# Two more of the seven outer products of three down groups by inner products, h sums and x added by accumulating transfers

## The chip, the cores and the metric

The kernel runs on one core of a Trainium2 chip. The metric is the device time of one execution, in microseconds. The core has five engines that run their own instruction streams and wait for each other by semaphores: TensorE (PE in the profile, with its weight loads as PEld), VectorE (DVE), ScalarE (ACT), GpSimd (POOL) and SyncE (SP), which in this kernel only issues transfers. Matmuls write to PSUM, which has 8 banks of 128 x 512 float32 numbers.

## The reference

```python
def _A_ref(x, wqkv, wo):                      # linear attention, 32 heads of 32
    qkv = (x @ wqkv) ...                      # S = 2048, D = 1024
    phi = lambda t: jnp.where(t > 0, t + 1, jnp.exp(t)) + 1e-6
    pq, pk = phi(q), phi(k)
    kv = jnp.einsum("bhsd,bhse->bhde", pk, v)
    z = jnp.einsum("bhsd->bhd", pk)
    num = jnp.einsum("bhqd,bhde->bhqe", pq, kv)
    den = jnp.einsum("bhqd,bhd->bhq", pq, z)[..., None] + 1e-6
    return (num / den) ... @ wo
def _B_ref(x, w_gate, w_up, w_down):          # F = 3584
    return (_silu(x @ w_gate) * (x @ w_up)) @ w_down
x = A_x
xn = _layernorm(x, axis=-1)
s = _A_ref(xn, A_wqkv, A_wo)
g = _silu(_B_ref(xn, B_w_gate, B_w_up, B_w_down))
return x + s * g
```

Inputs and output are bfloat16. The last matrix product, h @ w_down with h = silu(gate) * up, is the one that the change is about; below it is called the down product.

## The kernel before

**Seven products instead of eight.** Every large matrix product is computed as in Strassen's scheme (Winograd's form): both operands are cut into 2 x 2 blocks, seven products of sums of blocks are made, and the four output blocks are sums of these. The products are numbered 1 to 7. Products 1, 2 and 4 take raw blocks of the stationary operand; 5, 6, 7 and 3 take the sums S5, S6, S7 and S3 in the code's names. The moving operand has raw blocks `R00` to `R11` and sums `T1` to `T4`; the table `XOF` says which goes with which number. A `Set` holds the two PSUM banks and the side tiles in which the four output blocks of 128 rows x 512 columns come together: `put1`, `keep1`, `put2`, `put5`, `sum5` and `step` copy or add products out of PSUM with ACT and DVE. Two sets, `w` = 0 and 1, form a `Pair`.

**Inner products.** Some of the outer products are cut once more: a `Joint` makes one outer product for both sets of the pair by seven smaller products with 256 moving columns, in four steps a, b, c, d. Step a makes 1 and 5, b makes 6 and 2, c makes 7 and 3, d makes 4. In the step lists a word such as `7_0` is outer product 7 of set 0 in plain form, `j2c` is step c of the joint product 2, and a leading `n` means the next pair.

**Stages.** First come layer norm, transposes and the k and v products (to some 110 us), then, as pairs over the two halves `p` of the tokens, the q columns and seven column blocks `n` of the gate and the up weights, with the attention output s made in between. The gate's silu goes into a ring of eight tiles (`sg_ring`); for the up block the tile is multiplied in place (`h_done`) and stored to `h_scratch` in DRAM, four tiles (i, j) for each `p` and `n`. At about 534 us begin the four down groups of 512 tokens each (`Group`, `dset`). A group loads four blocks of h, makes S5, S7, S6 and S3 from them on DVE (`mk`), and multiplies with the down weights, whose raw blocks and sums stay in SBUF for all groups. Group 0 is plain; in groups 1 to 3 the products 1, 5 and 2 are joint, with inner sums of h by `inner_stat` for each group (the entries I1, I5, I2 of `todo`) and inner sums of the weights by `inner_move` once, during group 0. `evac` of `dset` ends each output block: ACT makes the silu, DVE multiplies with s (loaded from `s_scratch`), DVE adds x (loaded from the input), and SyncE stores the result. The last product of all, 4_1 of group 3, is made in three column pieces (`pieces`).

**What sets the order.** The host builds a list of operations with their reads and writes and a planner (`Plan.schedule`) orders each engine's list: an operation has a due time `dl` that is worked back from TensorE's order, `urgent` and `boost` move it forward, and at each point the engine takes what is due first among what is ready. TensorE keeps the written order, apart from taking a ready product up to ten operations ahead. `emit` turns the order into instruction streams with semaphore waits. Every name given to `dsem` is one DMA semaphore, and at the end SyncE waits for the final count of each of them. The planner's instructions stand in the profile under the line of the helper that makes them: L230 is every matmul, L237 every transpose, L360 ACT, L370 DVE's tensor_tensor, L373 a transfer on SyncE, L222 a wait.

Of the kernel before, what the change touches and what calls it, by code (L numbers as in the profile page):

```python
# [30 lines left out]
class Plan:  # L31
# [60 lines left out]
    def schedule(self):  # L92
# [29 lines left out]
        while len(order) < total:  # L122
# [37 lines left out]
            if o.sem is not None:  # L160
                free[e] = s + 0.08
# [79 lines left out]
def build_kernel(nc, A_x, A_wqkv, A_wo, B_w_gate, B_w_up, B_w_down, out, WINDOW=10, NWARM=14, NPE=4, LEAD=16.0, CLAMP=1000.0, AHEAD=4.0):  # L241
# [12 lines left out]
    with ExitStack() as es:  # L254
# [27 lines left out]
        TM = Arena("TM", 14 * KB)  # L282
        ident = sbt("ident", [128, 128], FP16)
        ones = sbt("ones", [128, 128], FP16)
        maskbd = sbt("maskbd", [128, 128], FP16)
        Zh = sbt("Zh", [128, NG, 32], FP16)
# [3 lines left out]
        stats = sbt("stats", [128, 4, 2, 6], F32)  # L290
# [7 lines left out]
        h_scr = nc.dram_tensor("h_scratch", [4, 2, 2, 128, NPAIR, 256], FP16)  # L298
# [76 lines left out]

        class Ring:
# [29 lines left out]
        ident_r, ones_r, mask_r, nh_r, eps_r = (named(n) for n in ("ident", "ones", "mask", "nh", "eps"))  # L406
# [81 lines left out]
        class Set:  # L488
# [4 lines left out]
            def __init__(self, ops, evac):  # L493
                self.ops, self.evac, self.direct = ops, evac, None
                self.pieces = ()
# [25 lines left out]
            def put2(self, b):  # L521
                if self.direct is not None:
# [8 lines left out]
            def sum5(self):  # L531
                self.c = balloc()
# [3 lines left out]
            def put5(self, e):  # L536
                self.s5 = s5_ring.take()
                act([bank_r[e]], [self.s5.r], self.s5.ap(F32), ps[e][:, :], ACT.Identity)
                bfree(e)

# [78 lines left out]
        class Pair:  # L619
# [6 lines left out]
            def do(self, w):  # L626
# [8 lines left out]
                for fn in self.at.get({"j2c": "2_0", "j2d": "2_1"}.get(w), ()):  # L635
# [5 lines left out]
        LINK2 = ("nj1a nj5a j2d nj1b nj5b 7_0 4_0 nj1c nj2a 3_1 nj2b nj5c n6_0 7_1 nj5d nj1d 4_1 nj2c n3_0 n6_1"  # L641
                 ).split()
# [6 lines left out]
        def feed(pair):  # L649

            prev = last_pair[0]
            if pair is None or not pair.joint:
                if prev is not None:
                    for w in (REST if "2" in (prev.joint or ()) else TAIL):
# [5 lines left out]
            else:  # L660
                third = [x is not None and "2" in (x.joint or ()) for x in (prev, pair)]
                l2 = LINKD if pair.down else LINK2
                link = LINK if not third[1] else l2 if third[0] else LINK1
                early = REST[:6] if third == [True, False] else [w[1:] for w in l2] if third[0] else ()
# [3 lines left out]
                for w in link:  # L668
                    if w[0] == "n":
                        pair.do(w[1:])  # L670
                    elif prev is not None and w not in prev.did and (w[0] != "j" or "2" in prev.joint):
# [38 lines left out]
        def ln_tile(i):  # L710
# [6 lines left out]
            if i == 1:  # L717
                for o in (o0, o1):
                    o.preds.add(first_var[0])
                    first_var[0].succs.append(o)  # L720
            dve([sA, sB], [mvr], lambda h: h.bn_aggr(mv[:, j, :], stats[:, j, :, :]), 60)
# [7 lines left out]
            if i < 2:  # L729
                for c in (0, 512):  # L730
                    dve([s.r, mvr, rsr], [o.sub(2 * c, KB).r], lambda h, c=c: h.tensor_scalar(  # L731
                        oa[:, c:c + 512], xa[:, c:c + 512], mv[:, j, 0:1], rstd[:, j, :], ALU.subtract, ALU.mult),
                        512, 2.6).urgent = 100.0 - c / 25 - 40 * i
# [85 lines left out]
        KSPLIT = {(0, 1), (2, 1), (0, 0), (2, 0), (1, 0), (1, 1), (3, 1), (5, 1), (3, 0), (5, 0)}  # L819
# [289 lines left out]
        def inner_move(v, kt, at, raw=False, ms=(1, 5, 2)):  # L1109
# [3 lines left out]
            for m, places in zip(ms, at):  # L1113
# [3 lines left out]
                if raw and m != 5:  # L1117
# [15 lines left out]
        SPLIT = {(1, 0, 1, 1), (0, 0, 0, 1), (1, 1, 0, 1), (1, 1, 1, 0), (0, 0, 1, 1), (1, 0, 0, 1), (1, 1, 0, 0), (1, 0, 0, 0), (0, 0, 1, 0), (1, 0, 1, 0)}  # L1133
        RECIP = ((("q", 1, 1), "6_0"), (("g", 2, 0), "6_0"))
        NORM = [(("q", 1, 1), "6_1"), (("g", 1, 0), "2_1"), (("u", 1, 0), "6_0"), (("u", 1, 1), "2_1"), (("u", 2, 0), "6_0"), (("u", 2, 1), "6_0"), (("g", 3, 1), "6_0"), (("u", 3, 0), "6_1")]
# [3 lines left out]
        def joint_of(jstat, xin, n, s0, s1):  # L1139
# [6 lines left out]
            js = {"5": Joint(ops(5), lambda w, b: (s0, s1)[w].put5(b))}  # L1146
            if 2 in xin or n == 7:
# [46 lines left out]
        def recip(p):  # L1194

            db = balloc_part()
            mms, rd = [], [zh_r]
# [46 lines left out]

        sgs = {}
# [11 lines left out]
        def gu_pair(p, kind, n, stats, at):  # L1257
            stat, jstat = stats

# [13 lines left out]
            def h_done(w, i, j):  # L1273
                if w == 0:
# [3 lines left out]
                g = 2 * p + j  # L1278
                dma([s.r], [named("h", g, i, n)], h_scr[g, :, i, :, 2 * n:2 * n + 2, :].rearrange(
                    "h p n t -> p h (n t)"), s.ap(FP16).rearrange("p (h x) -> p h x", h=2),  # L1280
                    dsem("hs%d" % s.k), 256 * KB)

            def ev_u(w):
                def f(i, j, ap, r, bank):
                    o, orr = part(h_slot(i, j), w)
                    act([r], [orr], o, halves(ap), ACT.Identity)
# [85 lines left out]

        def wd_load(nm, urgent):
            k, j = DRAW[nm]
            _, rs, v = DV["T1" if nm == "R01" else nm]
            dma([], rs, v.bitcast(BF16), wd_v[:, k, :, j * 512:(j + 1) * 512], dsem("wd" + nm),
                1792 * KB).urgent = urgent
# [6 lines left out]
        def wd_sum(o, a, b):  # L1384
# [362 lines left out]
```

## Time and profile before

| | us |
|---|---|
| median of 3 runs (lowest, highest) | 707.46 (707.27, 707.83) |
| the profiled execution's own time | 707.21 |
| its span, first to last instruction | 705.5 |
| PE busy | 697.2 |
| DVE busy | 602.8 |
| ACT busy | 420.9 |
| POOL busy | 13.5 |

The span leaves out 1.7 us of the profiled execution that lie around it. In the rows below, a group row reads: line, engine, operation, output <- inputs, shapes, count, then busy time and mean duration in ns, then idle time before it and what ended that. A timeline row begins with the start and the length in us. A matmul's row is longer than its share of the time, because matmuls overlap: the distance from one start to the next is what counts.

### The profile page before, as it was taken

How to read it: one execution, taken by the hardware profiler on the slowest of the kernel's cores; microseconds unless marked ns; L12 is line 12 of the kernel's file. 1: busy time of each engine (PE TensorE's matmuls, PEld its weight loads, DVE VectorE, ACT ScalarE, POOL GpSimd, SP SyncE). 2: the span in 40 equal slices, each digit the busy share in tenths (PEclk: the TensorE clock that was granted, in tenths of full speed). 3: DMA queues.
4: the chain of work that ended last, by engine and by line, in shares of the span. 5: the costliest groups of instructions: out<-in, count | busy, mean ns of one | idle time of the engine just before them, and what ended most of it. 6: DMA issues, size and time to landing. Idle time of an engine off the chain costs nothing.

```text
span 705.5 us, 11626 instructions
## 1 busy us (share of the span) xinstructions
PE 697.2 (99%) x4286; PEld 409.3 (58%) x4311; DVE 602.8 (85%) x1391; ACT 420.9 (60%) x834; POOL 13.5 (2%) x35
## 2 busy tenths in 40 slices
PE   8999999999999999999999999999999999999997
PEld 3544445555555666666666666666664457575754
DVE  6999997667999899898999999779899997766853
ACT  4887545877978868688786577775762122222212
POOL 2111000000000000000000000000000000000000
PEclk9999999999999999999999999999999999999999
DMA  9454113113112325343430252749443754446423
GB/s 308 110 112 99 30 60 120 61 60 122 57 61 87 98 91 154 88 145 96 151 119 1 76 192 85 230 142 317 134 151 134 220 175 158 142 139 226 136 66 93
DMA packets 87161, 88.98 MB, mean 126 GB/s; under 512 B 17728, under 2 KB 83008, under 8 KB 87104
## 3 DMA queue, kind: packets, MB, share of 16 engines
q1 hardware_dynamic: 87104, 88.23, 40.4%
q8 instruction: 34, 0.56, 0.3%
q14 instruction: 23, 0.19, 0.1%
HBM read 61.87 MB, written 23.20 MB: 121 GB/s over the span
## 4 chain that ended last, share of the span: by engine, by line
PE 97%; DVE 1%; DMA 0%; ACT 0%; issue 0%
PE ps L230 97%; DMA W<-in_A_x_dram 0%; DVE W L370 0%; PE ps L237 0%; DVE stats L715 0%; DVE H L808 0%; DVE stats L716 0%; DVE TM L370 0%; ACT X L360 0%; ACT TM L360 0%; ACT H L360 0%; DVE TM L807 0%; ACT ps L360 0%; DVE W L731 0%; ACT W L360 0%
## 5 line engine op out<-in xcount | busy, mean ns | idle before, releaser
L230 PE MATMUL ps<-P,W 128*128 128x512 f16 (+1 forms) x952 | 200.1, 341 | 0.0
L360 ACT ACTIVATE TM<-ps 128x512 f32<-128x512 f32 (+2 forms) x331 | 165.2, 532 | 51.7 <-PE ps L230 50.3
L370 DVE TENSOR_TENSOR ps<-ps,TM 128x256 f32<-128x256 f32 (+1 forms) x304 | 148.2, 508 | 54.9 <-PE ps L230 48.9
L230 PE MATMUL ps<-X,W 128*128 128x512 f16 (+1 forms) x896 | 187.9, 340 | 0.1
L360 ACT ACTIVATE H<-ps 128x512 f16<-128x512 f32 (+1 forms) x181 | 106.7, 601 | 62.5 <-PE ps L230 61.2
L230 PEld LDWEIGHTS ps<-P,W 128*128 128x128 f16 (+1 forms) x952 | 93.1, 98 | 65.5 <-issue 0.2
L230 PEld LDWEIGHTS ps<-X,W 128*128 128x128 f16 (+1 forms) x896 | 87.5, 98 | 58.3
L370 DVE TENSOR_TENSOR W<-W 128x256 f16<-128x256 bf16 (+4 forms) x274 | 98.1, 395 | 12.4 <-ACT W L360 8.9
L230 PE MATMUL ps<-H,W 128*128 128x512 f16 (+3 forms) x475 | 105.6, 357 | 0.8
L360 ACT ACTIVATE ps<-ps 128x256 f32<-128x256 f32 (+2 forms) x143 | 61.5, 430 | 56.7 <-PE ps L230 50.1
L230 PE MATMUL ps<-W 128*128 128x256 f16 x533 | 93.6, 273 | 0.0
L370 DVE TENSOR_TENSOR H<-H 128x1024 f16<-128x1024 f16 (+5 forms) x149 | 85.7, 593 | 7.3 <-ACT H L360 7.2
L230 PE MATMUL ps<-H,X 128*128 128x512 f16 (+4 forms) x383 | 74.3, 340 | 0.6 <-ACT X L360 0.4
L230 PEld LDWEIGHTS ps<-H,W 128*128 128x128 f16 x490 | 47.5, 98 | 45.1 <-ACT TM L360 0.3
L370 DVE TENSOR_TENSOR TM<-ps,TM 128x512 f32<-128x512 f32 x93 | 63.6, 685 | 10.2 <-PE ps L230 9.5
L230 PEld LDWEIGHTS ps<-W 128*128 128x128 f16 (+1 forms) x533 | 52.1, 98 | 29.3 <-ACT TM L360 0.5
L230 PEld LDWEIGHTS ps<-H,X 128*128 128x128 f16 x388 | 36.6, 98 | 32.1 <-ACT X L360 0.5
L230 PE MATMUL ps<-H 128*128 128x256 f16 (+4 forms) x386 | 54.5, 272 | 0.2
L360 ACT ACTIVATE H<-TM 128x512 f16<-128x512 f32 x61 | 38.2, 630 | 8.0 <-DVE TM L370 7.3
L230 PEld LDWEIGHTS ps<-H 128*128 128x128 f16 (+1 forms) x390 | 34.2, 98 | 13.9 <-ACT H L360 0.2
L370 DVE TENSOR_TENSOR H<-ps,TM 128x512 f16<-128x512 f32 (+1 forms) x59 | 40.2, 685 | 2.2 <-PE ps L230 1.8
L230 PE MATMUL ps<-W,H 128*128 128x256 f16 (+1 forms) x230 | 41.9, 317 | 0.0
(89 smaller groups left out, 471.9 us busy)
## 6 DMA issues: line engine op xcount, KB each, us to landing
h_scratch<-H SPq DMA_DIRECT2D x56, 256.0 KB, 3.2
W<-in_B_w_gate_dram SPq DMA_DIRECT2D x7, 1024.0 KB, 5.3
W<-in_B_w_up_dram SPq DMA_DIRECT2D x7, 1024.0 KB, 5.9
H<-in_B_w_down_dram SPq DMA_DIRECT2D x4, 1792.0 KB, 9.1
X<-h_scratch SPq DMA_DIRECT2D x7, 896.0 KB, 5.3
W<-h_scratch SPq DMA_DIRECT2D x5, 896.0 KB, 5.2
W<-in_A_x_dram SPq DMA_DIRECT2D x16, 256.0 KB, 3.2
H<-in_A_wqkv_dram SPq DMA_DIRECT2D x8, 512.0 KB, 8.3
```

The lines of the kernel that those rows point to most:

```text
L230: last = h.matmul(o, l, r, start=st, stop=sp, skip_group_check=True)
L360: op = PL.op("act", reads, writes, lambda h: h.activation(o, i, func, **kw), nel(o) / 1200.0 + (0.055 if src == "ps" else 0.095))
L370: return dve(reads, writes, lambda h: h.tensor_tensor(o, a, b, op), nel(o), 1.92 if fast else 0.96)
```

## The change

- **Joint products.** In groups 1 to 3 the outer products 6 and 3 are joint as well, besides 1, 5 and 2. `Set` gets `third`, `put6` and `put3`; the product sums go through SBUF tiles instead of a third bank. Inner sums I6 and I3 are added for each of these groups, and two more `inner_move` once. The step lists of the down groups (`LINKD`, `RESTD`) are new.
- **Roles exchanged.** In the down product h takes the sums in another arrangement, and the table `DOF` replaces `XOF` for it: the blocks of h are 00, 5, 10, 7 and 11, with 6 = 7 - 00 and 4 = 10 - 6 made by DVE. The tile (0, 1) of h is stored nowhere by itself; it is negated when it is made.
- **h sums by transfers.** Tile (0, 0) is stored twice, as 00 and as 5; tile (1, 1) twice, as 11 and 7; tile (1, 0) once. Tile (0, 1) is then added in DRAM to 5 and to 7 by accumulating transfers, which GpSimd issues (`dacc`).
- **x by transfers.** For groups 0 to 2 six transfers copy x into the output beforehand, and the finished product is added to it by an accumulating transfer. Group 3 keeps the old form, with eight tiles for s and for x.
- **Placement and times.** h slots go from 6 to 4; `ident`, `ones`, `maskbd`, `Zh` and `stats` move into the TM arena; the down weights are loaded in halves, each held back until the third one before it has landed. One warm-up matmul less; at the start the second half of tile 1's statistics comes behind tile 0's normalising. Some jobs (`SPLIT`, `NORM`, `BUILD`) have other places, and the table `BOOST` shifts the due times of some 80 operations. The planner counts a transfer's issue time by its engine.

```diff
-    def build_kernel(... NWARM=14 ...)
+    def build_kernel(... NWARM=13 ...)
...
+        def dacc(reads, writes, o, i, s, nbytes):
+            return PL.op("pool", reads, writes, lambda h: h.dma_start(o, i, accum_op=ALU.add), 1.0, sem=s, nbytes=2 * nbytes)
...
             def keep1(self, a):
-                self.b = a
                 self.s1 = s1_ring.take()
                 act([bank_r[a]], [self.s1.r], self.s1.ap(F32), ps[a][:, :], ACT.Identity)
+                if self.third:
+                    bfree(a)
+                else:
+                    self.b = a
+            def put6(self, b):
+                self.b = b
+                tt([bank_r[b], self.s1.r], [bank_r[b]], ps[b][:, :], ps[b][:, :], self.s1.ap(F32), ALU.add)
+                self.sum5()
...
+            def put3(self, b):
+                d = self.c
+                tt([bank_r[b], d.r], [d.r], d.ap(F32), ps[b][:, :], d.ap(F32), ALU.add)
+                bfree(b)
+                self.evac(0, 1, d.ap(F32), d.r, None)
...
-        LINK2 = ("... nj5d nj1d 4_1 nj2c n3_0 n6_1"
+        LINK2 = ("... nj5d nj1d 4_1 n3_0 nj2c n6_1"
-        LINKD = ("7_0 3_0 nj1a nj1b 7_1 nj5a nj5b 3_1 nj1c nj1d nj2a 4_0 nj5c nj2b nj5d n6_0 4_1 nj2c n6_1 nj2d"
+        LINKD = ("7_0 7_1 j3a j3b 3_0 j3c 4_0 j3d 4_1 3_1 nj1a nj1b nj5a nj5b nj1c nj5c nj1d nj2a nj5d nj2b nj6a nj2c nj6b nj6c nj2d nj6d"
+        RESTD = "j3a j3b 7_0 j3c 4_0 7_1 j3d 4_1".split()
...
             if i == 1:
-                for o in (o0, o1):
-                    o.preds.add(first_var[0])
+                for o, p in ((o0, first_var[0]), (o1, first_var[-1])):
+                    o.preds.add(p)
...
+            if n == 7:
+                js["3"] = Joint(ops(3), lambda w, b: (s0, s1)[w].put3(b))
+                js["6"] = Joint(ops(6), lambda w, b: (s0, s1)[w].put6(b))
...
-                dma([s.r], [named("h", g, i, n)], h_scr[g, :, i, ...], ..., dsem("hs%d" % s.k), 256 * KB)
+                if (i, j) != (0, 1):
+                    for q, nm in enumerate(HAT[i, j]):
+                        r, to = place(nm)
+                        dma([s.r], [r], to, tile(s), dsem("hs%d_%d" % (s.k, q)), 256 * KB)
+                for q, (nm, at) in enumerate((("5", (0, 0)), ("7", (1, 1)))):
+                    if (0, 1) in h_out and at in h_out and (i, j) in ((0, 1), at):
+                        r, to = place(nm)
+                        t = h_out[0, 1]
+                        dacc([t.r, r], [r], to, tile(t), dsem("ha%d_%d" % (t.k, q)), 256 * KB)
...
-        hslots = Slots([(X, 0), (X, 7 * KB), (X, 14 * KB), (X, 21 * KB), (W, 38 * KB), (W, 45 * KB)], 7 * KB)
+        hslots = Slots([(X, 0), (X, 7 * KB), (X, 14 * KB), (X, 21 * KB)], 7 * KB)
-        (g_ring of 3, sl_ring of 3, xo_ring of 4)
+        (g_ring of 3, sl_ring of 2, se_ring of 8, xo_ring of 8)
...
-                self.todo = ["L00", "I1", "L01", "L11", "S5", "I5", "S7", "L10", "S6", "I2", "S3"]
+                self.todo = ["L00", "I1", "L5", "I5", "L10", "I2", "L7", "S6", "I6", "S4", "L11", "I3"]
...
                     act([r], [q.r], qa, ap, ACT.Silu, "ps" if bank is not None else "sb")
                     tt([q.r, tr], [q.r], qa, qa, ta, ALU.mult, True)
+                    if self.g < 3:
+                        dacc([q.r, named("ox", self.g, i)], [named("oo", row, j)], of[row:row + 128, cols], qa,
+                             dsem("oa%d" % q.k), 128 * KB)
+                        return
                     tt([q.r, xr], [xr], xa, qa, xa, ALU.add, True)
                     dma([xr], [], of[row:row + 128, cols], xa, dsem("oo%d_%d" % (x.k, c0)), n * 128)
...
+        for g in range(3):
+            for i in range(2):
+                row = 1024 * (g // 2) + 512 * i + 256 * (g % 2)
+                dma([], [named("ox", g, i)], of[row:row + 256, :], xf[row:row + 256, :], dsem("ox%d%d" % (g, i)),
+                    512 * KB).urgent = 250.0
...
+        for k, v in BOOST.items():
+            PL.ops[k].boost = v
```

More of the change, by code (lines that the diff above doesn't have):

```diff
@@ L160, in schedule @@
             if o.sem is not None:
-                free[e] = s + 0.08
+                free[e] = s + o.busy
                 t0, rate, t1 = self.ALONE if o.start < self.RUSH else self.MIXED
@@ L281, in build_kernel @@
         W = Arena("W", 52 * KB)
[L282 to L286, printed above, removed]
+        TM = Arena("TM", 15 * KB + 512)
+        ident, ones, maskbd = (TM.at(14 * KB + 256 * q, 256, FP16) for q in range(3))
+        Zh = TM.at(14 * KB + 768, 512, FP16).rearrange("p (g n) -> p g n", n=32)
         hmask = sbt("hmask", [128, 4], F32)
@@ L403, in sub @@
                 return Slot(self.a, self.off + off, n, self.k)
-        ident_r, ones_r, mask_r, nh_r, eps_r = (named(n) for n in ("ident", "ones", "mask", "nh", "eps"))
+        ident_r, ones_r, mask_r = (TM.reg(14 * KB + 256 * q, 256) for q in range(3))
+        nh_r, eps_r = named("nh"), named("eps")
         def pool(reads, writes, fn, busy=0.3):
@@ L531, in sum5 @@
             def sum5(self):
+                if self.third:
+                    d = self.c = s1_ring.take()
+                    tt([bank_r[self.b], self.s5.r], [d.r], d.ap(F32), ps[self.b][:, :], self.s5.ap(F32), ALU.add)
+                    return
                 self.c = balloc()
@@ L661, in feed @@
                 third = [x is not None and "2" in (x.joint or ()) for x in (prev, pair)]
-                l2 = LINKD if pair.down else LINK2
-                link = LINK if not third[1] else l2 if third[0] else LINK1
-                early = REST[:6] if third == [True, False] else [w[1:] for w in l2] if third[0] else ()
+                link = LINKD if pair.down else LINK if not third[1] else LINK2 if third[0] else LINK1
+                early = () if pair.down else REST[:6] if third == [True, False] else [w[1:] for w in LINK2] if third[0] else ()
                 for w in REST:
@@ L1285, in f @@
                     o, orr = part(h_slot(i, j), w)
[L1286 removed]
+                    act([r], [orr], o, halves(ap), ACT.Identity, scale=-1.0 if (i, j) == (0, 1) else 1.0)
                     h_done(w, i, j)
```

198 lines of the change are left out of this document (102 added, 96 removed), and 7 rows, old and new, of the table BOOST.

## The prediction

> **What bounds the kernel now.** I read the page first, then the windows, then TensorE's timeline, because the share of busy time says little where matmuls overlap.
>
> ```profile
> span 705.5 us, 11626 instructions
> PE 697.2 (99%) x4286; PEld 409.3 (58%) x4311; DVE 602.8 (85%) x1391; ACT 420.9 (60%) x834; POOL 13.5 (2%) x35
> PE 97%; DVE 1%; DMA 0%; ACT 0%; issue 0%
> 270.00:400.00 130.00, 130.00 (x837) 81.80 (x836) 121.99 (x290) 95.34 (x203) 0.00 (x0) 1.00 0.34 105
> 534.00:591.00 57.00, 56.74 (x311) 30.70 (x315) 56.17 (x94) 12.39 (x24) 0.00 (x0) 1.00 0.44 140
> 591.00:605.00 14.00, 14.00 (x89) 8.54 (x89) 9.06 (x18) 2.23 (x4) 0.00 (x0) 1.00 0.54 179
> 605.00:700.00 95.00, 94.68 (x601) 58.45 (x606) 60.49 (x126) 22.42 (x44) 0.00 (x0) 1.00 0.46 144
> ```
>
> The third line is the chain that ended last, by engine: 97% of it is TensorE. The window rows give length, then busy time of PE, PEld, DVE, ACT and POOL, the granted clock and the DMA share. The clock is 1.00 in each row and PE is never idle by more than 0.4 us a stage, which missing records explain. So from the first product on, the time is the sum of the matmuls; every other engine matters only where it runs late. One engine is close to that: DVE, with 121.99 of 130 us in the gate/up stage and 56.17 of 57 at the start of the down groups.
>
> **The gain: TensorE's work.** Two kinds of product stand side by side in the third down group:
>
> ```profile
> 657.33 0.93 PE L230 MATMUL ps<-H,X 128*128 128x256 f16 x7
> ...
> 661.92 0.93 PE L230 MATMUL ps<-W,X 128*128 128x256 f16 x7
> 662.68 3.19 PE L230 MATMUL ps<-H,X 128*128 128x512 f16 x14
> ...
> 671.05 3.18 PE L230 MATMUL ps<-P,X 128*128 128x512 f16 x14
> 674.07 3.19 PE L230 MATMUL ps<-H,X 128*128 128x512 f16 x14
> 677.09 0.93 PE L230 MATMUL ps<-W,H 128*128 128x256 f16 x7
> ```
>
> Seven groups of 7 narrow matmuls (657.33 to 661.92, then 662.68) take 5.35 us from start to start; that is one whole product done by inner products, 49 of 256 columns. A plain outer product is two groups of 14 wide ones: 671.05 to 677.09, 6.04 us. The change turns products 3 and 6 of groups 1, 2 and 3 from the second kind into the first: 6 x (6.04 - 5.35) = **4.1 us less**. PE has no slack to give this back to, so it is a real gain unless something runs late. Group 0 stays plain. That the edit does less than it says is no case: the new schedule lists hold j3 and j6, and both are built for every group with inner sums.
>
> **The end gets longer.** The last instructions are SyncE's waits, one for every DMA semaphore:
>
> ```profile
> 701.87 0.43 SPq L373 DMA_DIRECT2D out_dram<-TM  x1
> L222 SPq EVENT_SEMAPHORE  x39: 17/28/28, 702.3 to 705.0; - x39
> ```
>
> The second row is line 222 on SyncE in the window 702 to 706. The kernel before uses 78 DMA semaphores (my count of the names), so 39 instructions carry two waits each, and they run one after another from 702.3 to 705.0: 2.7 us over 38 steps, 0.07 us each, all after the last DMA was issued. The names of the new version count to 118: stores of h 8 to 14 and accumulates into h 8 new, loads of h 10 to 8, down weights 4 to 8, s tiles 3 to 10, x tiles 4 to 8, output stores 6 to 10, x copies 6 new, accumulates into the output 3 new; the other 43 stay. That is 20 more instructions on the end, **+1.3 us**. The bounds are 0, if waits already met cost nothing or go elsewhere, and 1.6, if the chain also stalls a second time.
>
> **The last product.** The end order becomes 7_0, j3c, 4_0, 7_1, j3d, 4_1. The last one is cut into column pieces, and its first piece waits for a DVE sum and two ACT copies out of the bank that 7_1 fills:
>
> ```profile
> 691.47 3.19 PE L230 MATMUL ps<-H,X 128*128 128x512 f16 x14
> 691.67 0.69 DVE L370 TENSOR_TENSOR TM<-ps,TM 128x512 f32<-128x512 f32 x1 [1.51 <-PE ps L230]
> 692.40 0.56 ACT L360 ACTIVATE ps<-ps 128x128 f32<-128x128 f32 x2 [3.15 <-DVE TM L370]
> 697.52 3.25 PE L230 MATMUL ps<-H,X 128*128 128x256 f16 x42
> ```
>
> 7_1 gives way at 691.47, the copies are done at 692.96: 1.5 us. Before, 6 us of products covered that. Now only j3d stands behind 7_1, 5.35 / 7 = 0.76 us, so up to 0.8 us of stall. It is 0 if the planner's order of the ready products puts another one there. I take **+0.4**.
>
> **The start.** The normalising of tile 0 no longer queues behind the second half of tile 1's statistics:
>
> ```profile
> 5.46 0.56 POOL L725 TENSOR_TENSOR rstd<-veps,neg_half 128x1 f32<-128x1 f32 x1 [1.50 <-DVE veps L722]
> 6.02 0.68 DVE L716 BATCH_NORM_STATS2 stats<-W 128x6 f32<-128x512 bf16 x1
> 6.61 0.72 DVE L731 TENSOR_SCALAR W<-W,mv,rstd 128x512 f16<-128x512 bf16 x2
> 8.31 0.73 DVE L731 TENSOR_SCALAR W<-W,mv,rstd 128x512 f16<-128x512 bf16 x2 [0.67 <-POOL rstd L725]
> 7.07 0.72 PE L237 MATMUL ps<-ident,W 128*128 128x128 f16 x8 [0.47 <-DVE W L731]
> 8.15 1.04 PE L230 MATMUL ps<-H,X 128*128 128x512 bf16 x4 [0.37 <-ACT X L360]
> 9.03 0.61 PE L237 MATMUL ps<-ident,W 128*128 128x128 f16 x8
> ```
>
> rstd is there at 6.02, so the first product can come up to 0.5 us sooner. But tile 1's normalising then moves from 8.31 to about 8.5, and the transposes at 9.03 wait for it, so most of that is lost again. Bounds -0.5 and 0; I take **-0.1**. The one warm-up matmul less ends in the gap before 7.07 and costs nothing; with that gap gone it would be what the clock loses, which no row here shows.
>
> **The sums moved to transfers.** DVE's pieces for this, and the transfers' own:
>
> ```profile
> L370 DVE TENSOR_TENSOR X<-X 128x1024 f16<-128x1024 f16 x24 | 15.7, 683 | 0.2 <-PE ps L230 0.2
> L370 DVE TENSOR_TENSOR W<-H 128x1792 f16<-128x1792 bf16 x3 | 3.2, 1081 | 0.0
> L370 DVE TENSOR_TENSOR H<-X 128x896 f16<-128x896 f16 x12 | 7.3, 617 | 0.0
> L370 DVE TENSOR_TENSOR TM<-W,TM 128x512 bf16<-128x512 f16 x31 | 12.9, 421 | 0.6
> L370 DVE TENSOR_TENSOR ps<-ps,TM 128x256 f32<-128x256 f32 x18 | 7.7, 429 | 18.0 <-PE ps L230 18.0
> L373 SPq DMA_DIRECT2D h_scratch<-H x56: 359/371/4482, 162.8 to 554.1; - x56
> DMA to landing us min/median/max: 2.1/4.1/10.8
> ```
>
> Per group DVE loses S5 and S7, 2 x (3 x 0.68 + 0.42) = 4.9 us, and in groups 0 to 2 the adding of x, 8 x 0.42 = 3.4. It gains, in groups 1 to 3, inner sums for 6 and 3 (8 x 0.62 = 4.9), four full-width sums (4 x 0.69, from the 691.67 row) and four of 256 columns (1.7): 9.4 against 8.3, about even. Once, around group 0, come 8 block sums of 1.08, 8.6 us. Groups 0 and 1 together: 2 x 8.3 off, 9.4 + 8.6 on, +1.4 us against 4.9 idle in 591 to 605. It fits, but DVE has no pause before 591, so a sum can come late: bounds 0 and 1.0 us, I take **+0.2**. ACT's extra copies fall into 2.23 of 14 and 22.42 of 95 us busy.
>
> On SyncE, stores of h go from 56 to 70 and loads from 16 to 20, 0.37 us of issue each. The down weights come as eight halves instead of four, six copies of x to the output are added, and 24 x loads and 24 output stores go. That is fewer in all, and an earlier place in the queue for those behind. The six copies and the added h traffic cost nothing while the DMA share is 0.34 to 0.54; without that room they would delay a weight load by one landing, at most 10.8 us.
>
> The new waits are POOL's. Each accumulate stands in POOL's queue until the store that it adds to has landed; behind it are only other accumulates. Who waits for them: the loads of 5 and 7, a group later, and ACT, whose silu of the next gate reuses the tile. The second is tight:
>
> ```profile
> 346.48 0.43 SPq L373 DMA_DIRECT2D h_scratch<-H  x1
> 359.11 1.82 SPq L373 DMA_DIRECT2D h_scratch<-H  x2
> 363.49 1.89 PE L230 MATMUL ps<-X,W 128*128 128x512 f16 x8
> 364.55 0.60 ACT L360 ACTIVATE H<-ps 128x512 f16<-128x512 f32 x1 [0.31 <-PE ps L230]
> 374.98 1.89 PE L230 MATMUL ps<-P,W 128*128 128x512 f16 x8
> ```
>
> Of a pair's four stores the third is that of tile (1,1), which the last accumulate adds to; it is issued at 346.48 for the first half of the tokens, and the tile that is added, (0,1), is written again at 364.55: 18.1 us. For the second half it is 359.11 to about 376.0 (374.98 and the same 1.06): 16.9 us. A store and an accumulate in a row are 8.2 us at the median landing and 21.6 at the worst. No row shows an accumulate; its bounds are the fastest and slowest plain transfer, 2.1 and 10.8, and I take 5, nearer the median. Cost 0, because 4.1 + 5 fits into 16.9. The Trainium skill, "DMA: Bandwidth & Descriptors", Latency and other measured facts, gives a transfer begun by GpSimd about 1 us to its first byte against 0.6 us for SyncE's. By that the sum would be the same, and no run here shows it yet.
>
> The due-time offsets and the moved small jobs change no count of matmuls; PE has no idle time for them to win, so they are 0, or a loss already bounded above.
>
> **Sum.** -4.1 + 1.3 + 0.4 - 0.1 + 0.2 = -2.3. The profiled execution took 707.21 us (its span 705.5 and 1.7 around it): 704.9. The runs' median, 707.46, is 0.25 above it, so **705.1**. With the kinder bounds (-0.5 at the start, no stall, 1.2 at the end) 704.1; with the worse ones (1.6, 0.8, 0, 1.0) 706.8.
>
> **Rivals.** *A, the end does not grow* and nothing stalls: 707.46 - 4.1 - 0.1 = 703.3. For it: waits already met are short (28 ns in the row). Against: they step by 0.07. *B, DVE is late* around group 1: each us by which its backlog outlasts PE's is lost whole, and 1 to 3 of them give 706.1 to 708.1. For it: 56.17 of 57. Against: 4.9 idle right behind. *C, slower: the accumulate is late.* It decides where store plus accumulate pass 16.9 us. Each us beyond stops ACT in order, and with it the banks, at six gates of the second half: 6 us per us over. With 2 us over: 705.1 + 12 = 717. Against it: 7 us of room. *D, slower: building the transfers holds DVE up.* In 270 to 400 DVE has 8.0 us free. A gate/up column lasts 46 us there (342 to 388 by its stores) and brings four accumulates, 11 in the window, so 0.7 us each is free. Above that DVE becomes the bound; at 1.2 us, 28 x 0.5 = 14 us, 719. No row shows POOL at work beside DVE in this stage. The Trainium skill, "SBUF — State Buffer", Who interferes with whom, speaks against this change: GpSimd shares DVE's second port pair, and a DVE instruction with two SBUF inputs contends with a GpSimd instruction that reads SBUF. It adds that one which only writes does not contend, and descriptors are written; by that D stays small.
>
> **Chances.** About 0.2%, 1.4 us, is what these runs tell from no change, so faster is below 706.05 and slower above 708.9. Forecast 0.62 (own range 703.9 to 706.0), A 0.10, B 0.13, C 0.10, D 0.05. Faster 0.72, same 0.13, slower 0.15. The range 703.1 to 708.2 takes in the first three and leaves out C, D and the ends, a little under 2 in 10.
>
> **What would show it.** Right: 42 groups of 7 narrow matmuls in place of 12 of 14 wide ones, 126 matmuls more; line 222 on SyncE about 59 times after the last DMA; PE busy without gaps from 534 on but for some tenths before the last pieces. Wrong: ACT's silu waiting for a DMA into h_scratch (C), DVE operations longer than the means above (D), PE idle in groups 1 to 3 behind DVE (B), or still 39 waits (A).

## The result and the profile after

| | before | after |
|---|---|---|
| median of the runs, us (lowest, highest) | 707.42 (707.17, 707.84) | 704.53 (704.40, 704.77) |
| the profiled execution's own time | 707.21 | 704.51 |
| its span | 705.5 | 702.7 |
| TensorE's last matmul ends at | 700.77 | 696.74 |
| span behind that | 4.73 | 5.96 |

The changed kernel is faster: the ratio of after to before is 0.9961, with a 95% interval of 0.995 to 0.9971. Six runs of each stand behind it.

The page of the profile after, and the same windows as before (length, busy time of PE, PEld, DVE, ACT and POOL, granted clock, DMA share, GB/s):

```profile
span 702.7 us, 11996 instructions
PE 694.8 (99%) x4436; PEld 421.4 (60%) x4436; DVE 610.7 (87%) x1391; ACT 424.7 (60%) x848; POOL 68.4 (10%) x87
PE 99%; ACT 0%; POOL 0%; DVE 0%; issue 0%; POOLq 0%
270.00:400.00 130.00, 130.00 (x838) 81.82 (x837) 122.79 (x289) 94.55 (x202) 11.97 (x10) 1.00 0.57 148
534.00:591.00 57.00, 57.00 (x317) 30.82 (x316) 53.54 (x80) 12.10 (x22) 10.47 (x11) 1.00 0.71 185
591.00:605.00 14.00, 14.00 (x124) 11.88 (x122) 11.62 (x22) 3.77 (x9) 1.70 (x2) 1.00 0.42 104
605.00:700.00 95.00, 91.74 (x708) 67.77 (x706) 69.11 (x141) 25.21 (x54) 11.89 (x14) 1.00 0.60 167
```

TensorE still carries the chain, now 99% of it, at a clock of 1.00 in each window; the last window holds 3.26 us without it because the last matmul ends earlier. There are 150 matmul records more than before, where 126 were announced: behind the first product the trace of before has 25 steps that are one wide matmul, 0.216 us, too long, where a record is missing, and that of after has none; with one warm-up matmul less, 126 - 1 + 25 = 150. DVE has become freer at the start of the down groups, 53.54 of 57 us where it had 56.17, and S5, S7 and the adding of x are no longer made there. POOL has gone from 13.5 to 68.4 us: it now issues 52 accumulating transfers.

Where the time came from can be read at two points. TensorE's first product starts 0.22 us sooner (7.93 against 8.15), its last matmul ends 4.03 us sooner, and the end behind it is 1.23 us longer. In between stand two new pauses of TensorE, 0.12 us behind the matmul at 10.95 (a load of weights ends it) and 0.15 behind the one at 681.82 (a DVE sum ends it). So the matmuls themselves got shorter by 4.03 - 0.22 + 0.27 = 4.08 us, and the whole span by 4.03 - 1.23 = 2.8.

The beginning and the end of TensorE's timeline (start, length, then the instructions; in brackets the idle time before and what ended it), what DVE and ACT did for the last product, and SyncE's waits at the end:

```profile
1.43 5.59 PE L230 MATMUL ps<-TM 128*128 128x512 f16 x13 [1.43 <-POOL TM L415]
6.85 0.61 PE L237 MATMUL ps<-TM,W 128*128 128x128 f16 x8
7.93 2.80 PE L230 MATMUL ps<-H,X 128*128 128x512 bf16 x12 [0.47 <-ACT X L358]
...
685.15 4.71 PE L230 MATMUL ps<-P,X 128*128 128x512 f16 x21
689.70 3.19 PE L230 MATMUL ps<-H,X 128*128 128x512 bf16 x14
692.72 0.93 PE L230 MATMUL ps<-TM,X 128*128 128x256 f16 x7
693.48 3.25 PE L230 MATMUL ps<-H,X 128*128 128x256 bf16 x42
...
689.90 0.69 DVE L368 TENSOR_TENSOR TM<-ps,TM 128x512 f32<-128x512 f32 x1 [0.49 <-PE ps L230]
690.62 0.56 ACT L358 ACTIVATE ps<-ps 128x128 f32<-128x128 f32 x2 [0.88 <-DVE TM L368]
...
L222 SPq EVENT_SEMAPHORE  x59: 17/28/28, 698.4 to 702.2; - x59
```

TensorE's 7_1 gives way at 689.70, and what follows is 4_0 (bf16, H and X, 14 matmuls), not j3d. The DVE sum and the ACT copies at 689.90 and 690.62 are done long before the last step of j3 and the column pieces at 693.48 need the bank. Line 222 stands on SyncE 59 times, 39 before.

### The profile page after: what moved, and what is told of

The parts are those of the page before. It is cut to its first block, busy times and chain, and to the rows that moved or that the text cites. A ratio compares the mean times of both kernels' runs of the same rounds, so it can differ in the third digit from the quotient of the medians.

```text
span 702.7 us, 11996 instructions
## 1 busy us (share of the span) xinstructions
PE 694.8 (99%) x4436; PEld 421.4 (60%) x4436; DVE 610.7 (87%) x1391; ACT 424.7 (60%) x848; POOL 68.4 (10%) x87
## 4 chain that ended last, share of the span: by engine, by line
PE 99%; ACT 0%; POOL 0%; DVE 0%; issue 0%; POOLq 0%
PE ps L230 99%; PE ps L237 0%; ACT X L358 0%; DVE W L368 0%; POOL TM L415 0%; ACT W L358 0%; POOL TM L414 0%; POOLq L1792 0%
## 5 line engine op out<-in xcount | busy, mean ns | idle before, releaser
L368 DVE TENSOR_TENSOR ps<-ps,TM 128x256 f32<-128x256 f32 (+1 forms) x322 | 157.7, 509 | 40.2 <-PE ps L230 35.8
L230 PE MATMUL ps<-P,W 128*128 128x512 f16 (+1 forms) x896 | 188.9, 338 | 0.0
L230 PEld LDWEIGHTS ps<-P,W 128*128 128x128 f16 (+1 forms) x896 | 87.6, 98 | 58.4 <-DVE ps L368 0.2
L230 PE MATMUL ps<-H,X 128*128 128x512 bf16 (+4 forms) x556 | 104.8, 336 | 0.5 <-ACT X L358 0.5
L368 DVE TENSOR_TENSOR W<-W 128x256 f16<-128x256 bf16 (+6 forms) x256 | 89.1, 388 | 5.1 <-PE ps L230 2.9
L230 PEld LDWEIGHTS ps<-H,X 128*128 128x128 f16 x556 | 52.8, 98 | 41.6 <-ACT X L358 0.6
L375 POOL DMA_DIRECT2D h_scratch<-H x28 | 33.7, 1283 | 437.4 <-DVE H L368 197.0
L230 PE MATMUL ps<-H,W 128*128 128x512 f16 (+2 forms) x280 | 63.6, 358 | 0.0
L230 PE MATMUL ps<-H 128*128 128x256 f16 (+4 forms) x432 | 60.9, 273 | 0.0
L230 PE MATMUL ps<-W,H 128*128 128x256 f16 (+1 forms) x314 | 53.5, 305 | 0.0
```

The source lines that it names most:

```text
L230: last = h.matmul(o, l, r, start=st, stop=sp, skip_group_check=True)
L368: return dve(reads, writes, lambda h: h.tensor_tensor(o, a, b, op), nel(o), 1.92 if fast else 0.96)
L375: return PL.op("pool", reads, writes, lambda h: h.dma_start(o, i, accum_op=ALU.add), 1.0, sem=s, nbytes=2 * nbytes)
```

## The experiments

All ratios are against the kernel before, run on the same chip.

**1 and 2: what do the final waits cost?** Both kernels get an end that waits only for the transfers into the output; every other transfer has been waited for by its reader.

```diff
-        for s in semn.values():
-            if id(s) in PL.count:
+        for nm, s in semn.items():
+            if id(s) in PL.count and nm[:2] in ("oo", "oa"):
```

> The changed kernel, but SyncE waits at its end only for the 13 semaphores of transfers that write the output, not for all 118. Theory (the change lengthened the end by 20 waits, +1.2 us, and all 59 stand in a row after the last issue): the waits end with the last landing, 699.41 in the changed kernel's trace, and about 0.4 us of closing follow, so the span falls by 2.7 to 2.9 us and the time to about 701.7. Rival (the end is set by the last landing or by something behind the waits): no change, 704.5.

> The kernel before, with final waits for the semaphores of the output stores alone, 6 of 78. Theory: the last landing is at 703.40 in its trace, the waits end at 705.10, so the time falls by 1.5 to 1.7 us, to about 705.8. The distance from this to the changed kernel with the same short end is then the change without its end: 4.0 to 4.2 us, matmuls and start. Rival (the end costs nothing in either): 707.4, and the distance stays 2.9.

The changed kernel with the short end: 701.71 us (701.36 to 702.07), ratio 0.9921 (0.9905 to 0.9938). The kernel before with it: 706.01 (705.47 to 706.68), ratio 0.9981 (0.9972 to 0.9991). Line 222 on SyncE, first of the changed kernel, then of the kernel before:

```profile
L222 SPq EVENT_SEMAPHORE  x6: 27/28/28, 698.4 to 699.5; - x6
...
L222 SPq EVENT_SEMAPHORE  x3: 17/28/28, 703.1 to 703.7; - x3
```

The waits begin at the same 698.4 as in the changed kernel and end 2.7 us sooner; the time falls by 2.8. In the kernel before it falls by 1.2 to 1.4 (that kernel took 707.23 in this series and 707.42 in the first). Without both lists the two kernels are 4.30 us apart, with them 2.9, so the longer list costs 1.4 us of the change's gain. The 4.30 are about TensorE's 4.1 and the start. Rival A is out: waits that have long been met do cost time, each its step of 0.06 to 0.07 us. The first of these two is also the fastest kernel of this study.

**3: are the due-time offsets worth nothing?** The table `BOOST` is left out.

```diff
-        for k, v in BOOST.items():
-            PL.ops[k].boost = v
```

> The changed kernel without the table of offsets to due times. Theory (TensorE's work alone makes the gain, the offsets at most remove small waits): 704.5 to 707, with the same number of matmuls and a few gaps on TensorE. Rival (the offsets make the gain): 707 or more, the whole 2.9 us lost.

706.47 us (705.82 to 707.66), ratio 0.9992 (0.9982 to 1.0001): the offsets bring some 2 us of the 2.9 (1.9 by the medians, 2.2 by the two ratios). In TensorE's timeline the time stands as pauses in the down groups, each with what ended it:

```profile
633.47 0.72 PE L230 MATMUL ps<-W,H 128*128 128x256 f16 x5 [0.53 <-DVE ps L368]
...
662.65 0.94 PE L230 MATMUL ps<-W,H 128*128 128x256 f16 x7 [0.87 <-ACT TM L358]
...
691.85 3.19 PE L230 MATMUL ps<-P,X 128*128 128x512 f16 x14
694.87 0.93 PE L230 MATMUL ps<-TM,X 128*128 128x256 f16 x7
696.12 3.27 PE L230 MATMUL ps<-H,X 128*128 128x128 bf16 x42 [0.32 <-ACT ps L358]
```

From start to start these steps are 0.69, 1.03 and 0.48 us longer than the matmuls need, and one more, behind the matmul at 671.73, is 0.20: 2.4 us in all. The first lies in group 2 and waits for a DVE sum, the second in group 3 and waits for an ACT copy. The last of them is the stall that the prediction priced at 0.4. Here only the last step of j3 stands between 7_1 and the column pieces, as the written list has it. With the offsets 4_0 is put there.

**4: products 3 and 6 plain, in the order of before.** On the kernel of experiment 3, 3 and 6 are outer products again, with the old step lists, three banks for a pair and six h slots. Transfers, placement and the exchanged roles stay.

```diff
-                js["3"] = Joint(ops(3), lambda w, b: (s0, s1)[w].put3(b))
-                js["6"] = Joint(ops(6), lambda w, b: (s0, s1)[w].put6(b))
...
-                st = Set(ops, evac, self.joint, -1.0)
+                st = Set(ops, evac, False, -1.0)
...
-        LINKD = ("7_0 7_1 j3a j3b 3_0 j3c 4_0 j3d 4_1 3_1 ..."
+        LINKD = ("7_0 3_0 nj1a nj1b 7_1 nj5a nj5b 3_1 nj1c nj1d nj2a 4_0 nj5c nj2b nj5d n6_0 4_1 nj2c n6_1 nj2d"
```

> As the kernel without offsets, but outer products 3 and 6 of all down groups plain again, with the step order, the two sets of banks and the six h slots of the kernel before; the h sums and x stay with accumulating transfers. Theory: 4.1 us more than the kernel without offsets (12 groups of 14 wide matmuls for 42 of 7 narrow ones), between 3.5 and 5.5 with other small gaps. Rival (the gain comes from the transfers that relieve DVE): within 1 us of it.

713.87 us (713.39 to 714.14), ratio 1.0093 (1.0078 to 1.0108): 7.4 more than experiment 3, and more than any theory had. One reason can be seen: in the order of before, with the new placement, DVE's sums come late in group 0:

```profile
561.60 0.93 PE L230 MATMUL ps<-H,W 128*128 128x256 bf16 x7
564.68 3.19 PE L230 MATMUL ps<-P,X 128*128 128x512 f16 x14 [2.15 <-DVE X L368]
```

With this step of 2.31 us, 0.64 behind the matmul at 551.67 and 1.9 before 340, the pauses come to 4.8 us, where experiment 3 has 2.6 (the 2.4 above and 0.2 at 331 to 335). That and a start that is 0.15 us later account for 2.4 of the 6.6 us by which the last matmul is later; 4.2 are left for the matmuls. The size is as forecast, but the run changes the order too, so it was made once more.

**5: the same with the new order kept.** Products 3 and 6 are plain but use the new side tiles and bank counts. In this order the sum of product 6 overwrites a side tile before product 2's sum has read it: block (0, 0) of groups 1 to 3 is made from other numbers, by the same operations. As in experiment 4, the inner sums that the joint forms of 3 and 6 need are left out with them; DVE is busy for 584.1 us, in experiment 3 for 610.1.

```diff
-        LINKD = ("7_0 7_1 j3a j3b 3_0 j3c 4_0 j3d 4_1 3_1 ... nj2a nj5d nj2b nj6a nj2c nj6b nj6c nj2d nj6d"
+        LINKD = ("7_0 7_1 3_0 4_0 3_1 4_1 ... nj2a nj5d nj2b n6_0 nj2c n6_1 nj2d"
-        RESTD = "j3a j3b 7_0 j3c 4_0 7_1 j3d 4_1".split()
+        RESTD = "3_0 7_0 7_1 4_0 3_1 4_1".split()
```

> The kernel without offsets, products 3 and 6 plain in all down groups, but now everything else of the change stays: the side tiles instead of a third bank, four h slots, the transfers, the same step order with plain words in the place of the joint ones. Theory: 4.1 us above the kernel without offsets (706.47), so 710.6, with gaps on TensorE that differ by no more than 1 us in sum. Rival (the plain form loses more because its order needs the six slots and three banks, or DVE has too little to do in time): 712 or more, with gaps that make up the difference. Rival (the joint form was no gain): 707.

709.55 us (709.40 to 710.26), ratio 1.0035 (1.0021 to 1.0048): 3.1 more than experiment 3, where 4.1 was expected. The two timelines settle the difference. In this kernel TensorE has no pause of over 0.1 us from 345 us on, but 0.8 us of them before, most at 319 to 336. In experiment 3 they are 2.6. So plain products save 1.8 us of pauses, and still the last matmul ends at 701.86 here and 699.38 there, 2.48 later: the matmuls alone are some 4.2 us longer, where the prediction's rows give 4.14. The 4.1 us are real. Without the offsets, the joint form makes sums on DVE and ACT late and loses over a third of them again; whether by its shorter products or by the 26 us of sums that it adds on DVE, no run tells.

**6 and 7: a late accumulate.** On the kernel of experiment 1, one or two plain transfers of 256 KB are put on POOL ahead of each of 24 accumulates into h. The copies share one place in DRAM.

```diff
+                            ce = named("copy", e)
+                            extras.add(PL.op("pool", [t.r, r] + cr, [ce], ...
...
-                        dacc([t.r, r], [r], to, tile(t), dsem("ha%d_%d" % (t.k, q)), 256 * KB)
+                        dacc([t.r, r] + cr, [r], to, tile(t), dsem("ha%d_%d" % (t.k, q)), 256 * KB)
```

> The changed kernel with the short end (701.71), and ahead of each accumulate into h of the first six column blocks one plain transfer of the same tile from GpSimd's queue to an unused place in DRAM, for whose landing the accumulate waits. Theory (the accumulate has 7 us of room or more before a silu needs its tile): no change, 701.3 to 702.3, and ACT waits for no such transfer. Rival (the accumulate is already at its limit): each delay of some 5.7 us shows at twelve gates, 20 us or more.

> The same with two such transfers, one after the other. A store (median landing 4.6 us) and three transfers of 5.7 us make 21.7 us against the 16.9 us after which the second half's tile is written again. Theory (ACT stops in order, the banks fill, TensorE stands): about 5 us over at six gates, up to 29 us, less what the banks cover, so 705 to 730, with TensorE's gaps behind ACT. Rival (the planner's order and the banks hide it): within 2 us of 701.7.

742.58 us (741.32 to 744.37), ratio 1.0501 (1.0484 to 1.0519), and 771.9 (767.63 to 773.86), ratio 1.0905 (1.0871 to 1.0938). The first is 41 us above experiment 1, which is where its rival had it (20 us or more); the second is above everything that was expected. But in the first ACT never waits for an accumulate, so the rival's reason is not what cost the time. POOL's timeline of the first shows an effect that was not meant:

```profile
312.89 0.76 POOL L1333 DMA_DIRECT2D c_scratch<-H  x1 [24.95 <-DVE H L371]
317.73 1.20 POOL L378 DMA_DIRECT2D h_scratch<-H  x1 [4.08 <-DMA c_scratch<-H]
322.42 0.76 POOL L1333 DMA_DIRECT2D c_scratch<-H  x1 [3.49 <-DMA h_scratch<-H]
327.06 1.20 POOL L378 DMA_DIRECT2D h_scratch<-H  x1 [3.89 <-DVE ps L371]
333.72 0.76 POOL L1333 DMA_DIRECT2D c_scratch<-H  x1 [5.46 <-DMA h_scratch<-H]
```

Copy and accumulate go one after another, each waiting for the landing of the one before, because all copies write one place and stand in one queue. Four such pairs fill 37 of the 46 us of a column. In the column before this one, the last accumulate goes out at 286.74, in experiment 1 at 266.73: not 5 but 20 us later. Only in the second kernel does ACT wait for an accumulate at all:

```profile
ACT H L361 <- DMA h_scratch<-H: 11.7, 5, 4.5
```

The columns are us in total, times and the longest: 11.7 us of the 70 lost. This is rival C's mechanism, seen on the chip, but most of the loss is something else. Part of it is TensorE's clock: the runs' mean granted clock is 0.984 to 0.991 with one copy and 0.969 to 0.973 with two, where experiment 1 has 1.0. Worked out from that, at most 7 to 12 us are lost with one copy and 21 to 24 with two. And TensorE waits for others: in the first kernel, for one, DVE waits 0.88 us for a load of up weights, then makes a block of 15 sums from it, and TensorE stands 3.9 us behind that block:

```profile
391.57 4.84 DVE L371 TENSOR_TENSOR W<-W 128x256 f16<-128x256 bf16 x15 [0.88 <-DMA W<-in_B_w_up_dram]
```

SyncE issued that load at 383.26, behind five stores of h at which it had stood since 373.06. The other pauses were not followed. So these two runs could not say how much room an accumulate has.

**8: fewer warm-up matmuls.** Experiment 1 with ten instead of thirteen.

```diff
-    def build_kernel(... NWARM=13 ...)
+    def build_kernel(... NWARM=10 ...)
```

> The changed kernel with the short end and 10 warm-up matmuls instead of 13. In the changed kernel's profile the full clock came at 6.5 us and the 13 warm-ups held TensorE until 6.85, while the first tile was normalised from 5.78 on; in the profile with the short end the clock came at 4.8 and the warm-ups were done ahead of the tile. Theory (in some executions the warm-ups hold the start): 0 to 0.5 us less than 701.71, 701.2 to 701.7, with a smaller spread. Rival (fewer warm-ups let the clock come later and the first products run at half speed): 0.2 to 1 us more.

702.32 us (702.14 to 703.19), ratio 0.9932 (0.992 to 0.9945): no gain, 0.6 more than experiment 1 in another series. The start, of this kernel and then of experiment 1:

```profile
1.44 4.12 PE L230 MATMUL ps<-TM 128*128 128x512 f16 x10 [1.44 <-POOL TM L415]
6.59 0.72 PE L237 MATMUL ps<-TM,W 128*128 128x128 f16 x8 [1.03 <-DVE W L756]
7.67 1.90 PE L230 MATMUL ps<-H,X 128*128 128x512 bf16 x8 [0.36 <-ACT X L358]
...
1.43 4.85 PE L230 MATMUL ps<-TM 128*128 128x512 f16 x13 [1.43 <-POOL TM L415]
6.51 0.72 PE L237 MATMUL ps<-TM,W 128*128 128x128 f16 x8 [0.23 <-DVE W L755]
7.60 1.90 PE L230 MATMUL ps<-H,X 128*128 128x512 bf16 x8 [0.37 <-ACT X L358]
```

In both the transposes wait for DVE's normalised tile and the first product for ACT's copy of them. Three warm-ups fewer only make TensorE wait 0.8 us longer. Of the 0.4 us by which the span is longer, 0.22 are there by the second set of transposes (10.97 against 10.75): 0.07 by the first product, the rest in a wait for a load of weights at 10.11 (0.54 us here, 0.39 there). What adds the other 0.2 is open.

**9 and 10: a late accumulate, made cleanly.** Each copy now goes out on SyncE and to a place of its own, so that nothing but the accumulate waits for it.

```diff
+                            ce = named("copy", e, p, nm, n)
+                            extras.add(dma([t.r] + cr, [ce], c_scr[e, p, HN[nm], n].rearrange("h p x -> p h x"),
+                                           tile(t), dsem("cp%d%d_%d" % (e, t.k, q)), 256 * KB))
...
-                        dacc([t.r, r], [r], to, tile(t), dsem("ha%d_%d" % (t.k, q)), 256 * KB)
+                        dacc([t.r, r] + cr, [r], to, tile(t), dsem("ha%d_%d" % (t.k, q)), 256 * KB)
```

> The version that waits only for the output's transfers, with one more store of 256 KB between the h sum and its accumulating transfer: each of the 24 accumulates of the first six column pairs now also waits for a plain transfer of the same tile from SP to a place of its own, which nothing else touches. The computation is the same. A plain store of 256 KB took a median of 3.2 us from issue to landing, so an accumulate lands 3 to 5 us later and the pair's tile comes free that much later. If there are 7 us of room behind an accumulate, as the prediction took from the rewrite of the tile, the time stays at that of the version without it, ratio 0.992 (0.991 to 0.994). If the 742.6 us with copies that shared one place came from there being no room at all, 24 delays of 3 to 5 us, two side by side, cost 12 x 4 = some 48 us at most, and half of that would show as 725 us, ratio 1.025.

> The same with two such stores, one behind the other: an accumulate lands 7 to 10 us later. If there are 7 us of room, this passes it by 0 to 3 us in each of 12 places: 702 to 738 us, with ScalarE or VectorE waiting for a transfer ahead of writing H in the trace. If the room is 10 us or more, the time stays at ratio 0.992. If there is none, the time goes up by twice what one store costs.

706.87 us (706.46 to 709.48), ratio 0.9996 (0.9986 to 1.0005), and 722.86 (719.99 to 723.46), ratio 1.0209 (1.0188 to 1.0231). That is 5.2 and 21 us above experiment 1, where 0 and 0 to 36 were expected. By the totals the first would speak against 7 us of room, but neither kernel shows a wait for an accumulate. POOL's accumulates of one column, first of experiment 1, then of the kernel with two copies, and DVE's and TensorE's rows of the latter:

```profile
249.98 1.18 POOL L375 DMA_DIRECT2D h_scratch<-H  x1 [68.65 <-DVE H L368]
255.51 1.19 POOL L375 DMA_DIRECT2D h_scratch<-H  x1 [4.35 <-DMA h_scratch<-H]
266.00 2.40 POOL L375 DMA_DIRECT2D h_scratch<-H  x2 [9.30 <-DVE H L368]
...
257.18 1.18 POOL L378 DMA_DIRECT2D h_scratch<-H  x1 [75.65 <-DMA c_scratch<-H]
263.35 1.19 POOL L378 DMA_DIRECT2D h_scratch<-H  x1 [4.99 <-DMA c_scratch<-H]
276.48 1.18 POOL L378 DMA_DIRECT2D h_scratch<-H  x1 [11.94 <-DMA c_scratch<-H]
...
DVE W L371 <- DMA W<-in_B_w_up_dram: 3.6, 2, 1.9
...
329.17 0.61 PE L230 MATMUL ps<-W 128*128 128x256 f16 x2 [2.81 <-DVE ps L371]
```

With two copies the accumulates of this column come 7 to 12 us later, and in neither kernel does ACT wait for one even once. Where the loss can be followed, it is the neighbour on SyncE: the load of up weights that experiment 1 issues at 312.8 leaves at 314.0 with one copy and at 317.5 with two. In the second case DVE waits 1.9 us for it, then makes its block of 15 sums, and TensorE stands 2.8 us behind that block. That is one of TensorE's pauses in this kernel; the others, some 7.7 us, were not followed. The clock has a part as well: 0.990 to 0.995 in the mean of the four executions, at most 4 to 7 us of the 21. With one copy nothing waits for the load itself, but TensorE's idle time stands at the same place, 320 to 341 us, where its order differs too; that part is argued, not shown.

These runs do not measure the room either, because the planner makes the order anew and the tile's next write moves along. The last accumulate of the column above lands at 275.99 in experiment 1 and at 283.88 with two copies, and ACT writes its tile again at 282.78 and at 291.47, though TensorE was only 0.4 us behind at 265. What the room is in an order as it stands can be read from the traces, as the time from an accumulate's landing to the first instruction that has to wait for it. In the changed kernel it is 6.3 us for the last accumulate of this column, but 2.9 for ACT at 508.03 (the accumulate issued at 498.25 landed at 505.12) and 1.9 for DVE at 401.96 (issued at 395.54, landed at 400.05). So the room is there, but it is 2 to 3 us at the tightest places, not 7; how much later an accumulate may come in a fixed order, no run tells.

## Why the prediction was right, point by point

- **TensorE's work, -4.1.** Measured -4.08 between the two traces, some 4.2 in experiments 4 and 5, and 4.30 between the two kernels with short ends, start included. The price from the rows of the third down group held.
- **The end, +1.3.** +1.23, and 59 waits as counted. Experiments 1 and 2 show it by taking it away. (20 steps at the prediction's 0.07 would be 1.4, not 1.3; in the changed kernel they take 0.065.)
- **The last product, +0.4.** It cost 0, its lower bound. The prediction took the stall from the written list of steps, and that step failed. With the offsets the planner puts 4_0 behind 7_1; without them the stall is there, 0.48 us.
- **The start, -0.1.** -0.22, and 0.12 of it is lost again at 10.95, so -0.1 in sum. The size is right by luck, for the reason was another: the prediction had tile 1's transposes wait for its late normalising, and they start at 10.56 without a wait. In the trace of after the thirteen warm-ups take 5.59 us and hold TensorE until 6.85, while tile 0 is normalised from 5.78; in experiment 1 they take 4.85, the transposes start at 6.51, and the gain is lost in the wait for a load at 9.88.
- **DVE late, +0.2.** One pause of 0.15 us, behind the matmul at 681.82, which a DVE sum ends.
- **The sum.** -4.08 - 0.22 + 0.27 + 1.23 = -2.8 where -2.3 was forecast: nearly all of the half microsecond is the last product. The medians differ by 2.9, and the 704.53 lies in the forecast's own range.
- **The offsets, 0.** The measured value is some 2 us (experiment 3). The prediction reasoned that TensorE has no idle time for them to win. That is true of the kernel before, and beside the point: the changed kernel without them has 2.4 us of idle time, and they take it out again. The total came right because the other terms had been priced as if nothing ran late; that they do not run late is the offsets' work. The prediction gave no reason for that, so here the total was right by luck: without the offsets, 706.47 lies above the forecast's own range.
- **The accumulates, 5 us each, hidden.** They are hidden. Their landing has a median of 5.7 us into h and 3.8 into the output; the store that they wait for has 3.2:

```profile
h_scratch<-H SPq DMA_DIRECT2D x70, 256.0 KB, 3.2
h_scratch<-H POOLq DMA_DIRECT2D x28, 256.0 KB, 5.7
out_dram<-W POOLq DMA_DIRECT2D x24, 128.0 KB, 3.8
L375 POOL DMA_DIRECT2D h_scratch<-H x28 | 33.7, 1283 | 437.4 <-DVE H L368 197.0 <-DVE ps L368 104.9 <-PE ps L230 95.6
```

  3.2 + 5.7 fits into 16.9, and rival C did not come. The 7 us of room that were held against it are wrong as a general figure: the tightest places have 2.9 us for ACT and 1.9 for DVE. The Trainium skill, "DMA: Bandwidth & Descriptors", Latency and other measured facts, has about 0.6 us to the first byte on SyncE's way and about 1 us on GpSimd's; the landings here are 2.5 us apart, and no run tells how much of that is the way and how much the adding.
- **Rival D, building the transfers.** POOL spends 1.2 us on each, more than the 0.7 beyond which D was to decide, and yet no loss shows on DVE. Its operations last as long as before, 685 and 426 ns here, 683 and 424 there over the whole trace. And those that run while POOL builds a transfer last no longer than the others: 686 ns for 12 of the wide sums below, 685 for the other 62; 425 for 26 of the narrow ones, 426 for the other 196.

```profile
L368 DVE TENSOR_TENSOR ps<-ps,TM 128x256 f32<-128x256 f32 x222 | 91.6, 426 | 26.1 <-PE ps L230 25.5
L368 DVE TENSOR_TENSOR H<-H 128x1024 f16<-128x1024 f16 x74 | 50.1, 685 | 7.5 <-ACT H L358 6.9
```

  The Trainium skill, "SBUF — State Buffer", Who interferes with whom, says that a DVE operation with two SBUF inputs contends with a GpSimd instruction that reads SBUF, not with one that only writes it, and infers that building a transfer only writes; the trace agrees.
- **Rival B, DVE late at group 1.** DVE's share at the start of the down groups fell, from 56.17 to 53.54 of 57 us, and TensorE has no pause there, not even without the offsets (53.40, experiment 3). What comes late without them comes in groups 2 and 3, and only the first of those pauses, 0.69 us before 633.47, is DVE's.

## What to carry to other kernels

Where one engine is busy without a pause, price a change by its work on that engine and read the price from start-to-start distances; that held here to 0.1 us. Then ask what the shorter work makes late, and compare any tuning of the order with the changed kernel without it, not with the kernel before. Count what is waited for at the very end: semaphores that nobody needs any more are instructions in a row behind the last transfer, and leaving them out was here worth as much as the whole change (2.8 and 2.9 us).

## What the runs showed of the hardware

Final waits cost 0.06 to 0.07 us each although nearly all of their transfers had landed long before: 59 of them take 3.8 us, 698.4 to 702.2.

TensorE lost its full clock without a long pause. In the trace of experiment 9 it was busy 1.83 of 3 us, with idle times of 0.3 to 0.8 between short groups, and soon after that the granted clock was 0.55 for 3 us, again while it had work:

```profile
333.00:336.00 3.00, 1.83 (x13) 0.75 (x10) 3.00 (x11) 2.14 (x6) 0.00 (x0) 1.00 0.00 0
337.00:340.00 3.00, 3.00 (x13) 1.49 (x11) 2.01 (x6) 1.92 (x4) 0.00 (x0) 0.55 0.04 8
```

The Trainium skill, "TensorE: Matmul & The Clock Gate", A second HAM failure mode: psum-queue depth-cycling, tells of such a fall where TensorE idles shortly and often between groups of matmuls; the trace agrees. The 3 us at 0.55 cost another 1.35 us of full-speed work, so a few short stalls in a row can cost more than their sum. This execution was the slowest of ten, at 709.48 us; eight of the ten have a mean clock of 1.0, so there the same kernel kept its speed.

The traces of experiments 6, 7, 9 and 10 tell what went before. In them the clock stays low for 3.41 us or a multiple of it, and of the 14 falls while matmuls were left, each came behind 3.41 us in which TensorE was busy 51% or less. In experiment 4 it was busy 53% of the emptiest such stretch, from 560.71 on, with the pause of 2.15 us, and the clock stayed at 1.00. So the busy share tells these cases apart, and the length of a pause does not. The border of about a half is an estimate from these traces: experiment 6 also has a stretch of 51%, from 409.2 on, behind which the clock stayed at 1.00.
